# A 64-byte read of every later x chunk, issued early on the GpSimd queue

## The chip, the cores and the metric

The kernel runs on one core of a Trainium2 chip. The metric is the device time of one execution in microseconds (us), median over runs. A run counts as "fast": for a one-core program this only means that it is not more than 1.5% above the fastest run of the same kernel. The profile of an execution covers a "span" that is about 1.7 us shorter than the timed figure. In the views, PE is TensorE, PEld its weight loads, DVE VectorE, ACT ScalarE, POOL GpSimd and SP SyncE; L186 is line 186 of the kernel, and x5 a count.

## The reference, cut to what matters

```
def reference(A_x, A_wqkv, A_wo, B_x, B_w1, B_w2, B_w3, B_w4, gate_w):
    x = A_x                                    # (1, 2048, 640), bfloat16
    g = sigmoid((x * gate_w).sum(-1, keepdims=True))
    a = linear attention over 32 heads of 20: q, k, v = x @ wqkv;  phi(t) = where(t > 0, t + 1, exp(t)) + 1e-6
    b = shifted-mixer block and MLP with two layernorms: w1, w2, w3, w4
    return g * a + (1 - g) * b
    # [cut: the bodies of a and b]
```

The rows of x are taken as 16 chunks of 128 rows. The first stage needs each chunk transposed (`xT`), as the stationary operand of k = x @ wk.

## The kernel before

The parts that matter are the loads at the start, GpSimd's set-up, and the k stage. `sp`, `aq` and `gq` issue DMAs from SyncE, ScalarE and GpSimd.

```python
    def load_x(c0, c1, q=sp):
        q.dma_start(x_sb[:, c0:c1, 0:D], x2[c0 * P:c1 * P, :].rearrange("(c p) d -> p c d", p=P))

    def load_xT(c0, c1):
        sp.dma_start_transpose(xT[:, :, c0 * P:c1 * P], x2[c0 * P:c1 * P, :])

    # [cut: load_wk loads 128 rows of wk]

    load_x(0, 1)
    aq.dma_start(g5[:], gate_w.rearrange("(c p) -> c p", p=P))
    load_wk(sp, 1)
    load_wk(aq, 0)
    load_x(1, 2, aq)
    load_wk(sp, 3)
    load_wk(aq, 2)
    load_wk(sp, 4)
    for c0, c1 in ((2, 3), (3, 4), (4, 6), (6, 8), (8, 12), (12, 16)):
        load_xT(c0, c1)
    sp.dma_start(wq_sb, wqkv_v[:, :, 0:D])
    load_x(2, 8)
    load_x(8, 16)
    sp.dma_start(wv_sb[:], wqkv_v[:, :, 2 * D:3 * D])
    # [cut: the loads of w1, wo, w2, w3]

    nc.gpsimd.memset(mhalf[:], -0.5)
    nc.gpsimd.memset(ident[:], 1.0)
    nc.gpsimd.affine_select(out=ident[:], in_=ident[:], compare_op=ALU.is_equal, fill=0.0,
                            base=0, pattern=[[-1, P]], channel_multiplier=1)
    nc.gpsimd.memset(x_sb[:, :, D:D + 1], 1.0)
    # [cut: other masks, kvT memsets, and copies that wait for w1]
```

Chunks 0 and 1 are loaded as they are and transposed on TensorE. Chunks 2 to 15 come through DMA transposes, in six loads of 1, 1, 2, 2, 4 and 4 chunks. The k stage fills the time of the first loads with warm-up matmuls on ones:

```python
    warmup(5)
    warmup(1, 3 * P)
    kp = pair()
    turns = [(pair(), a, b) for a, b in ((0, 2), (2, DC))]
    # [cut: turn(c) transposes chunk c on TensorE and evacuates it]
    turn(0)
    warmup(1, TS)
    for n, dc in enumerate(k0_order):
        if n == 3:
            turn(1)
        elif 1 <= n < 3:
            warmup(1, 2 * P)
        k_mm(kp, 0, (dc,), first=k0_order[0], last=k0_order[-1])
    k_evac(kp, 0)
    for c in range(1, NCH):
        pt = pair()
        k_mm(pt, c, range(DC))
        k_evac(pt, c)
```

The next stage (`q_unit`) reads `xT` and `wq_sb`; the one after it reads the plain `x_sb`.

Of the kernel before, what the change touches and what calls it, by code (L numbers as in the profile page):

```python
# [9 lines left out]
BF16 = mybir.dt.bfloat16  # L10
# [6 lines left out]
def kernel(  # L17
# [14 lines left out]
    P = 128  # L32
# [3 lines left out]
    NCH = S // P  # L36
# [18 lines left out]
    x2 = A_x.rearrange("b s d -> (b s) d")  # L55
# [5 lines left out]
    const = ctx.enter_context(tc.tile_pool(name="const", bufs=1))  # L61
# [24 lines left out]
    r4 = const.tile([H, NT, TS], BF16)  # L86
    ident = const.tile([P, P], BF16)
    g5 = const.tile([DC, P], BF16)
    g5z = const.tile([P, P], BF16)
    mhalf = const.tile([P, CPT], F32)  # L90
    hmask = const.tile([P, H], F32)
# [24 lines left out]
    sp, aq, gq = nc.sync, nc.scalar, nc.gpsimd  # L116
# [27 lines left out]
    for g in range(4):  # L144
# [6 lines left out]
    nc.gpsimd.memset(ident[:], 1.0)  # L151
    nc.gpsimd.affine_select(out=ident[:], in_=ident[:], compare_op=ALU.is_equal, fill=0.0,
                            base=0, pattern=[[-1, P]], channel_multiplier=1)
    nc.gpsimd.memset(x_sb[:, :, D:D + 1], 1.0)
    nc.gpsimd.memset(hmask[:], 1.0)
    nc.gpsimd.affine_select(out=hmask[:], in_=hmask[:], compare_op=ALU.is_ge, fill=0.0,
# [466 lines left out]
```

## Time and profile before

| | before |
|---|---|
| time, median of 3 runs before the change was run | 264.34 us (264.27 to 264.57) |
| span of the profiled run | 262.6 us |
| TensorE busy | 257.9 us, 98% |
| first k matmul, last k matmul (start) | 4.22 us, 27.29 us |
| chunks 8-11 of xT: landed, first needed | 16.44 us, 16.52 us |

The first fence is from the page of before: the busy time of the engines, two rows of the span in 40 equal slices (each digit is the busy share of a slice in tenths), and the two lines of the chain that ended last.

```profile
PE 257.9 (98%) x1719; PEld 160.0 (61%) x1738; DVE 142.7 (54%) x282; ACT 82.7 (31%) x123; POOL 20.2 (8%) x65
...
PE   8999999999999999999999999999999999999995
...
DMA  7999987016682566600132000051100051100011
...
PE 98%; issue 0%; DVE 0%
PE pp L500 22%; PE pp L467 21%; PE pp L186 9%; PE pp L315 8%; PE pp L451 8%; PE pp L420 8%; PE pp L349 8%; PE pp L243 8%; PE pp L199 1%; PE pp L387 1%; PE pp L475 1%; PE pp L509 1%; PE pp L368 1%; PE pp L258 0%; PE pp L216 0%
```

TensorE bounds the kernel: it is at 9 in all slices but the first and last, and the chain holds no DMA, although the DMA row is at 9 for the first slices. Busy DMA is not a cost where nobody waits for it.

The second fence is the waits view of before, the lines of TensorE that name a DMA or an evacuation (engine, tile, line, what it waited for; us in total, times, longest).

```profile
PEld L216 <- DMA x_sb<-in_A_x_dram: 0.5, 1, 0.5
...
PEld L186 <- DVE xT L219: 0.2, 1, 0.2
PEld L214 <- DMA x_sb<-in_A_x_dram: 0.2, 1, 0.2
```

All three are in the first 6.1 us. No line says that TensorE waited for an `xT<-in_A_x_dram` load, which is what the change is aimed at.

The third fence is the timeline of before, TensorE only, the k stage and its neighbours (start, length, engine, line, operation, tiles, shapes, count).

```profile
4.22 0.93 PE L186 MATMUL pp<-wk_sb,xT 128*128 128x320 bf16 x2
...
5.15 0.68 PE L186 MATMUL pp<-wk_sb,xT 128*128 128x320 bf16 x2
...
5.77 0.44 PE L186 MATMUL pp<-wk_sb,xT 128*128 128x320 bf16 x2
...
6.08 0.45 PE L214 MATMUL pp<-ident,x_sb 128*128 128x128 bf16 x5
...
6.44 21.14 PE L186 MATMUL pp<-wk_sb,xT 128*128 128x320 bf16 x154
...
27.42 4.91 PE L243 MATMUL pp<-xT,hsT 128*128 128x512 bf16 x21
```

From 6.44 us, 154 matmuls run without a break.

Two more readings are of the trace's records, not of a view. The semaphore events say when each load has landed: it raises its semaphore in 16 steps, and the last one counts. The DMA packet records say how long each packet took: a transposed chunk is 640 packets of 256 bytes, the median one 18 ns; but there are bursts in which 12 to 19 packets take from 0.16 to 2.0 us and end together (at 6.36, 9.5, 11.55, 11.95 and 16.35 us). These groups of slow packets are called bursts below.

### The profile page before, as it was taken

Reading aid. Unit: us, or ns where it says so; the run is one execution under the profiler, and the core shown is the slowest. Engines: PE = TensorE matmul, PEld = TensorE weight load, DVE = VectorE, ACT = ScalarE, POOL = GpSimd, SP = SyncE. Lnnn points to the kernel's source line nnn. Section 1 sums busy time; section 2 is a strip of 40 time slices with the busy share of each in tenths; the row PEclk is TensorE's granted clock in tenths of the full one; section 3 lists DMA queues with packets and bytes.
Section 4 is the critical chain, followed back from the end, with each engine's and each line's share of the span. In section 5 each row is a group of like instructions: output and inputs, shape, how many; then the busy total and the mean of one; then the engine's idle time right before and its main releaser. Section 6 shows DMA issues by size and latency. Waiting matters only on the chain.

```text
span 262.6 us, 4246 instructions
## 1 busy us (share of the span) xinstructions
PE 257.9 (98%) x1719; PEld 160.0 (61%) x1738; DVE 142.7 (54%) x282; ACT 82.7 (31%) x123; POOL 20.2 (8%) x65
## 2 busy tenths in 40 slices
PE   8999999999999999999999999999999999999995
PEld 4777555788755644555577555567565577555553
DVE  2788778899947998955403464413356223112132
ACT  1555554321166236522502222412131332142200
POOL 5000050012210040001000001000001000000000
DMA  7999987016682566600132000051100051100011
GB/s 204 197 171 379 364 248 304 0 27 125 125 99 58 111 121 167 235 0 2 25 75 77 25 0 2 0 100 52 50 0 2 1 100 52 50 0 2 0 50 50
DMA packets 45757, 23.98 MB, mean 91 GB/s; under 512 B 35114, under 2 KB 44970, under 8 KB 45738
## 3 DMA queue, kind: packets, MB, share of 16 engines
q1 hardware_dynamic: 45296, 23.22, 35.1%
q10 hardware_dynamic: 442, 0.49, 0.5%
q8 instruction: 13, 0.21, 0.4%
q14 instruction: 6, 0.05, 0.1%
HBM read 12.21 MB, written 2.62 MB: 56 GB/s over the span
## 4 chain that ended last, share of the span: by engine, by line
PE 98%; issue 0%; DVE 0%
PE pp L500 22%; PE pp L467 21%; PE pp L186 9%; PE pp L315 8%; PE pp L451 8%; PE pp L420 8%; PE pp L349 8%; PE pp L243 8%; PE pp L199 1%; PE pp L387 1%; PE pp L475 1%; PE pp L509 1%; PE pp L368 1%; PE pp L258 0%; PE pp L216 0%
## 5 line engine op out<-in xcount | busy, mean ns | idle before, releaser
L467 PE MATMUL pp<-lnxT,w_sb 128*128 128x512 bf16 x249 | 59.8, 379 | 0.6
L500 PE MATMUL pp<-w_sb,h 128*128 128x384 bf16 (+3 forms) x414 | 57.6, 299 | 0.2 <-issue 0.2
L469 ACT ACTIVATE h<-pp 128x1024 bf16<-128x1024 f32 (+1 forms) x28 | 26.9, 961 | 82.2 <-PE pp L467 82.2
L500 PEld LDWEIGHTS <-h 128*128 128x128 bf16 x416 | 38.3, 98 | 19.3 <-issue 1.1
L467 PEld LDWEIGHTS <-w_sb 128*128 128x128 bf16 x260 | 25.4, 98 | 26.8
L514 DVE SCALAR_TENSOR_TENSOR oc<-pp,omg,x 128x640 bf16<-128x640 f32 (+2 forms) x20 | 14.4, 748 | 45.1 <-ACT h2x L478 21.3
L454 DVE SCALAR_TENSOR_TENSOR x<-pp,gate,x 128x640 f32<-128x640 f32 x16 | 13.9, 868 | 29.4 <-PE pp L451 29.4
L178 ACT ACTIVATE e<-pp 128x640 bf16<-128x640 f32 (+1 forms) x26 | 21.5, 826 | 9.6 <-PE pp L243 9.6
L451 PE MATMUL pp<-m_sb,pqT 128*128 128x320 bf16 x160 | 24.3, 299 | 0.0
L420 PE MATMUL pp<-w_sb,hsT 128*128 128x320 bf16 x160 | 23.9, 299 | 0.0
L423 DVE TENSOR_TENSOR x<-pp,x_sb 128x640 f32<-128x640 f32 x16 | 13.1, 820 | 19.7 <-PE pp L420 19.7
L186 PE MATMUL pp<-wk_sb,xT 128*128 128x320 bf16 (+1 forms) x160 | 23.1, 303 | 0.0
L315 PE MATMUL pp<-x_sb,pk 128*128 128x320 bf16 (+1 forms) x160 | 22.0, 300 | 0.0
L243 PE MATMUL pp<-xT,hsT 128*128 128x512 bf16 x98 | 21.6, 379 | 0.1
L315 PEld LDWEIGHTS <-pk 128*128 128x128 bf16 x160 | 18.8, 117 | 3.2
L420 PEld LDWEIGHTS <-hsT 128*128 128x128 bf16 x160 | 15.7, 98 | 8.2
L451 PEld LDWEIGHTS <-pqT 128*128 128x128 bf16 x160 | 15.7, 98 | 7.7
L186 PEld LDWEIGHTS <-xT 128*128 128x128 bf16 x160 | 15.7, 99 | 6.5 <-DVE xT L219 0.2
L349 PE MATMUL pp<-lnxT,w_sb 128*128 128x512 bf16 x76 | 17.9, 379 | 0.2
L243 PEld LDWEIGHTS <-hsT 128*128 128x128 bf16 x100 | 11.8, 118 | 9.7
L285 POOL TENSOR_SCALAR rstd<-mv 128x4 f32<-128x4 f32 (+1 forms) x11 | 3.4, 312 | 153.6 <-DVE mv L291 153.6
L180 DVE SCALAR_TENSOR_TENSOR pk<-pp,e 128x640 bf16<-128x640 f32 x16 | 13.2, 825 | 1.7
(76 smaller groups left out, 189.9 us busy)
## 6 DMA issues: line engine op xcount, KB each, us to landing
out_dram<-oc SPq DMA_DIRECT2D x14, 160.0 KB, 1.8
w_sb<-in_B_w_dram SPq DMA_DIRECT2D x1, 2160.0 KB, 8.4
w_sb<-in_B_w_dram SPq DMA_DIRECT2D x1, 2080.0 KB, 9.9
x_sb<-in_A_x_dram SPq DMA_DIRECT2D x1, 1280.0 KB
x_sb<-in_A_x_dram SPq DMA_DIRECT2D x1, 960.0 KB, 7.4
wo_sb<-in_A_wo_dram SPq DMA_DIRECT2D x6, 160.0 KB, 7.8
hsT<-in_A_wqkv_dram SPq DMA_DIRECT2D x1, 800.0 KB, 5.1
m_sb<-in_A_wqkv_dram SPq DMA_DIRECT2D x1, 800.0 KB, 12.0
```

What stands on the lines that cost most here:

```text
L178: nc.scalar.activation(ev, src, ACT.Exp)
L186: nc.tensor.matmul(pt[:, hf, 0:n], lhsT=xT[:, dc, c * P:(c + 1) * P], rhs=wk_sb[:, dc, hf * HD:hf * HD + n], start=(dc == first), stop=(dc ...
L243: nc.tensor.matmul(pt[:, t % 2, :], lhsT=wq_sb[:, dc, :].rearrange("p (m j) -> p j m", j=DC)[:, j], rhs=xT[:, dc, t * TS:(t + 1) * TS], st ...
L315: nc.tensor.matmul(pt[:, hf, 0:HD + hf], lhsT=w, rhs=x_sb[:, c, hf * HD:(hf + 1) * HD + hf], start=(c == 0), stop=(c == NCH - 1))
L349: nc.tensor.matmul(pt[:, i, :], lhsT=w, rhs=lnxT[t][:, dc, :], start=(dc == 0), stop=(dc == DC - 1))
L420: nc.tensor.matmul(pt[:, hf, 0:HD], lhsT=hsT[:, fc, 2 + c * P:2 + (c + 1) * P], rhs=w2_sb[:, fc, hf * HD:(hf + 1) * HD], start=(fc == 0), ...
L451: nc.tensor.matmul(pt[:, hf, 0:HD], lhsT=pqT[:, j, c * P:(c + 1) * P], rhs=m_sb[:, j, hf * HD:(hf + 1) * HD], start=(j == 0), stop=(j == D ...
L454: nc.vector.scalar_tensor_tensor(x1, pt[:, :, 0:HD], gate[:, c:c + 1], x1, op0=ALU.mult, op1=ALU.add)
L467: nc.tensor.matmul(pt[:, k, :], lhsT=w3_sb[:, dc, fc * P:(fc + 1) * P], rhs=lnT[:, dc, :], start=(dc == 0), stop=(dc == DC - 1))
L469: nc.scalar.activation(h2[:, 2 * i * TS:(2 * i + n) * TS], pt[:].rearrange("p h e -> p (h e)")[:, 0:n * TS], ACT.Gelu_apprx_tanh)
L500: nc.tensor.matmul(dst, lhsT=st[t]["h2"][:, fc * TS + cc * P:fc * TS + (cc + 1) * P], rhs=w4_sb[:, fc, a:b], start=start and fc == 0, stop ...
L514: nc.vector.scalar_tensor_tensor(oc[:, a:b], src, omg[:, c:c + 1], st[t]["x1"][cc][:, a:b], op0=ALU.mult, op1=ALU.add)
```

## The change

Its intent, as the code suggests, is to read a little of every later x chunk while the first chunks are loading, so that whatever makes the first packets of those chunks slow is over by the time the transposed loads reach them. The spare tile is read by nothing.

```diff
@@
     g5 = const.tile([DC, P], BF16)
+    touch = const.tile([NCH - 2, 32], BF16)
     g5z = const.tile([P, P], BF16)
@@
     nc.gpsimd.affine_select(out=ident[:], in_=ident[:], compare_op=ALU.is_equal, fill=0.0,
                             base=0, pattern=[[-1, P]], channel_multiplier=1)
+    gq.dma_start(touch[:], x2.rearrange("(c p) d -> p c d", p=P)[0, 2:NCH, 0:32])
     nc.gpsimd.memset(x_sb[:, :, D:D + 1], 1.0)
```

## The prediction

> **What bounds the kernel.** TensorE. The page gives PE 257.9 us busy of a 262.6 us span (98%), and the chain that ended last is PE for 98%, with no DMA in it. From 6.44 us to the end the matmuls follow each other without a wait that the waits view lists above 0.4 us. Only the first 6.5 us are tied to loads. There the timeline shows PE and its weight load waiting 0.49 us for x chunk 0, 0.25 us for an evacuation of xT, and 0.20 us for x chunk 1; warm-up matmuls fill the rest.
>
> **What the loads look like now.** The semaphore events of the trace give landings. x chunk 1 has 15 of its 16 increments by 5.51 us and the last at 6.03; PE takes it at 6.08. The weight chunk needed next lands at 6.40 (used 6.44), the last one at 6.58 (used about 6.71). So start-up hangs on the loads within 0.05 to 0.15 us. The transposed loads of x chunks 2 to 15 all land before use: chunk 2 at 7.21 (first matmul 8.35), chunks 4-5 at 9.72 (11.07), 6-7 at 12.03 (13.80), 12-15 at 18.67 (21.97). The tightest is 8-11: landed 16.44, used 16.52, 0.08 us to spare. The packet records show bursts of slow packets where the transposes reach new chunks: a median 256-byte packet takes 18 ns, but some 18 of them at 5.8-6.2 us take 0.16 to 0.59 us, with further bursts at 9.0, 10.8, 11.7 and 14.3 us (up to 2.0 us). I read the change as an attempt to take these first-read delays early; that a first read is their cause is a guess.
>
> **What the change does.** It removes nothing. It adds one DMA of 14 x 64 bytes (896 bytes against 24 MB in total), issued from GpSimd after the identity mask, at about 1.35 us. Nothing reads the spare tile. It takes its own completion semaphore, so the built programs of the other engines have the same order and the same waits. GpSimd's remaining set-up (mask work and kvT memset, now done by 4.6 us) slips by the descriptor generation; the Trainium skill, "DMA: Bandwidth & Descriptors", section "Latency and other measured facts", gives about 1 us to first byte on this path. GpSimd then idles 28 us until w1 lands, so the slip is free. By the same page ("Issuing engines are not separate DMA queues") the 14 reads run on the same DMA engines as the start-up loads, so they reach them at an estimated 2.5-3.5 us, amid the weight and x chunk 1 loads.
>
> **On the critical path.** Gain: if the bursts at 5.8-6.2 us shrink, x chunk 1 and the last weight chunks land earlier, worth at most the 0.20 us wait plus about 0.1 us; and the chunk 8-11 load gets spare time that PE does not need. Earlier transposes otherwise buy nothing. Cost: slow first reads among the start-up loads could delay them by up to about 0.5 us, passed on one for one. Expected net: about -0.1 us.
>
> **Prediction.** 264.2 us, 263.6 to 264.8 (8 in 10). Faster by over 2%: 0.005; within 2%: 0.985; slower: 0.01.
>
> **Right or wrong in the profile.** Right: PE busy unchanged within 1 us; the slow packets at 9, 10.8 and 14.3 us fewer or shorter, chunk 8-11 landing before 16 us, yet the first q matmul (27.4 us now) within 0.4 us of its old place. Wrong: the bursts unchanged (the touch warms nothing), or x chunk 1 and the weights landing over 0.5 us later and the whole timeline shifted.
>
> **What would break it.** The load blocking a DMA engine for microseconds at start-up; a PE gap long enough to lower its clock; or a fixed cost outside the span for using the GpSimd queue at all (262.6 span against 264.34 timed).

## The result, and the profile after

| | before | after |
|---|---|---|
| time, median | 264.45 us (264.27 to 264.91, 4 runs) | 264.67 us (264.28 to 264.85, 4 runs) |
| ratio after / before | | 1.0004, 95% interval 0.9986 to 1.0021 |
| span of the profiled run | 262.6 us | 262.9 us |
| last k matmul (start) | 27.29 us | 27.48 us |
| chunks 8-11: landed, first needed | 16.44, 16.52 us | 14.79, 16.71 us |
| chunks 12-15: landed, first needed | 18.67, 21.97 us | 18.59, 22.16 us |

A ratio is the mean time of one kernel's fast runs over that of the other's of the same rounds, so it is not quite the ratio of the medians.

The page of after, the lines that answer to those of before, and the DMA queue that is new:

```profile
PE 258.1 (98%) x1719; PEld 160.3 (61%) x1738; DVE 142.7 (54%) x282; ACT 82.7 (31%) x123; POOL 20.7 (8%) x66
...
PE   8999999999999999999999999999999999999995
...
DMA  7999995016672566700132000051100051100011
...
q0 software_dynamic: 32, 0.00, 0.0%
...
PE 98%; issue 0%; DVE 0%
PE pp L502 22%; PE pp L469 21%; PE pp L188 9%; PE pp L317 8%; PE pp L453 8%; PE pp L422 8%; PE pp L351 8%; PE pp L245 8%; PE pp L201 1%; PE pp L389 1%; PE pp L477 1%; PE pp L511 1%; PE pp L370 1%; PE pp L260 0%; PE pp L218 0%
```

The chain is the same, shifted by two line numbers. The touch is 32 packets (14 of 64 bytes and 18 of 4 bytes); its share rounds to nothing.

GpSimd's timeline, one line of before and then those of after, shows what the touch costs there:

```profile
3.35 1.28 POOL L167 MEMSET kvT<- 128x320 bf16 x4
```

```profile
1.46 0.75 POOL L155 DMA_DIRECT2D touch<-in_A_x_dram  x1
2.21 0.19 POOL L156 MEMSET x_sb<- 128x16 bf16 x1
...
4.19 1.28 POOL L169 MEMSET kvT<- 128x320 bf16 x4
31.71 3.24 POOL L172 COPY w1x<-w_sb 128x32 bf16<-128x32 bf16 x20 [26.24 <-DMA w_sb<-in_B_w_dram]
```

Issuing takes GpSimd 0.75 us; the kvT memset starts at 4.19 us (3.35 before). Then GpSimd waits 26 us for w1 anyway. The DMA view gives 3.7 us from issue to landing, and the packet records put its 64-byte packets at 3.58 to 4.64 us.

TensorE's timeline of after:

```profile
4.31 0.85 PE L188 MATMUL pp<-wk_sb,xT 128*128 128x320 bf16 x2
...
5.16 0.74 PE L188 MATMUL pp<-wk_sb,xT 128*128 128x320 bf16 x2
...
5.91 0.60 PE L188 MATMUL pp<-wk_sb,xT 128*128 128x320 bf16 x2
...
6.35 0.44 PE L216 MATMUL pp<-ident,x_sb 128*128 128x128 bf16 x5
...
6.63 21.14 PE L188 MATMUL pp<-wk_sb,xT 128*128 128x320 bf16 x154
...
27.61 4.70 PE L245 MATMUL pp<-xT,hsT 128*128 128x512 bf16 x20
```

Two things differ. The unbroken run of 154 matmuls starts 0.19 us later and takes exactly as long (21.14 us). And, off TensorE's path, chunks 8-11 landed 1.65 us earlier. Is the second an effect of the touch, and the first its cost? One trace of each cannot tell. That is what the experiments are for.

### The profile page after: what moved, and what is told of

It reads as the page before. It is cut to its first block, busy times and chain, and to the rows that moved or that the text cites. A ratio compares the mean times of both kernels' runs of the same rounds, so it can differ in the third digit from the quotient of the medians.

```text
span 262.9 us, 4248 instructions
## 1 busy us (share of the span) xinstructions
PE 258.1 (98%) x1719; PEld 160.3 (61%) x1738; DVE 142.7 (54%) x282; ACT 82.7 (31%) x123; POOL 20.7 (8%) x66
## 4 chain that ended last, share of the span: by engine, by line
PE 98%; issue 0%; DVE 0%
PE pp L502 22%; PE pp L469 21%; PE pp L188 9%; PE pp L317 8%; PE pp L453 8%; PE pp L422 8%; PE pp L351 8%; PE pp L245 8%; PE pp L201 1%; PE pp L389 1%; PE pp L477 1%; PE pp L511 1%; PE pp L370 1%; PE pp L260 0%; PE pp L218 0%
## 5 line engine op out<-in xcount | busy, mean ns | idle before, releaser
L422 PEld LDWEIGHTS <-hsT 128*128 128x128 bf16 x160 | 15.7, 98 | 8.2
L453 PEld LDWEIGHTS <-pqT 128*128 128x128 bf16 x160 | 15.7, 98 | 7.7
```

What stands on the lines that cost most here:

```text
L422: nc.tensor.matmul(pt[:, hf, 0:HD], lhsT=hsT[:, fc, 2 + c * P:2 + (c + 1) * P], rhs=w2_sb[:, fc, hf * HD:(hf + 1) * HD], start=(fc == 0), ...
L453: nc.tensor.matmul(pt[:, hf, 0:HD], lhsT=pqT[:, j, c * P:(c + 1) * P], rhs=m_sb[:, j, hf * HD:(hf + 1) * HD], start=(j == 0), stop=(j == D ...
```

## The experiments

The theories:

- **A**: a 64-byte read of a chunk makes its later first reads quick, so the loads of 6-7 and 8-11 land earlier. The time is the same only because TensorE had no need of it.
- **B**: those landings move from run to run by themselves; the touch does nothing.
- **C**: the touch delays the start-up loads and costs about 0.2 us.
- **A'**: any extra DMA on GpSimd's queue does what the touch does.

Later came **F** (the longest burst belongs to the 16 KB fetch of TensorE's instructions), **I** (bursts come where a new transposed load begins) and **P** (bursts belong to places in x).

The first four kernels ran on one chip and share 7 runs of before there: 264.31 us (264.04 to 264.76).

### Before once more

No edit.

> The kernel before, unchanged, for the spread of its own landings. Theory A (a 64-byte read of a chunk makes the later first reads of that chunk quick): chunks 6-7 land again near 12.0 us and chunks 8-11 near 16.4 us (within 0.4 us), as in the first trace of before. Theory B (the bursts of slow packets come and go from run to run, whatever the touch does): these landings move by 0.7 us or more against the first trace, and could be as early as the 11.3 and 14.8 us that the changed kernel showed. Both expect a time within 0.1% of before.

Measured: 264.58 us (264.17 to 265.19, 4 runs), ratio 1.0009 (0.9986 to 1.0031). Chunks 6-7 landed at 11.52 us, 8-11 at 16.25. The last k matmul began at 27.59 us, 0.30 us later than in the first trace of the same kernel. So the start-up of one kernel moves by more than the 0.19 us between before and after. For chunks 6-7, A missed its 12.0 us by more than the 0.4 us that it allowed.

### After once more

No edit.

> The changed kernel, unchanged. Theory A: chunks 6-7 land again near 11.3 us and 8-11 near 14.8 us (within 0.4 us). Theory B: they land anywhere between 11.3 and 12.0, 14.8 and 16.5 us. Theory C (the touch delays the start-up loads): the last k matmul starts about 0.2 us later than in the traces of before (27.5 against 27.3 us) and the time is about 0.1% longer; if C is false, these lie within 0.1 us of those of before.

Measured: 264.47 us (264.14 to 264.65), ratio 1.0002 (0.9987 to 1.0017). Chunks 6-7 landed at 11.71 us, 8-11 at 15.10. The last k matmul began at 27.54 us, between the two traces of before. C is not seen. For 6-7 the touch no longer differs (11.71 us with, 11.52 without). For 8-11, A still stood at two traces against two.

### The touch, but from w4

```diff
-    gq.dma_start(touch[:], x2.rearrange("(c p) d -> p c d", p=P)[0, 2:NCH, 0:32])
+    gq.dma_start(touch[:], B_w4.rearrange("(c p) d -> p c d", p=64)[0, 0:NCH - 2, 0:32])
```

> The same extra load in the same place, 14 x 64 bytes, but from w4 (not needed before 100 us) in place of x. Theory A: no help, chunks 6-7 and 8-11 land as in before, near 12.0 and 16.4 us. Rival A' (any DMA on that queue, or the later GpSimd work, changes the bursts, not the addresses read): they land as in the changed kernel, near 11.3 and 14.8 us. Theory C: start-up as late as with the change. Time within 0.2% of before by all.

Measured: 264.39 us (264.18 to 264.77), ratio 1.0002 (0.9986 to 1.0017). Chunks 6-7 landed at 11.87 us, 8-11 at 16.05: as without a touch. So far for A, against A'. The last k matmul began at 27.06 us, earlier than in either trace of before although an extra DMA ran: against C, but weakly, since TensorE's full clock came early in this trace (below).

### A denser touch

Against the kernel after:

```diff
-    touch = const.tile([NCH - 2, 32], BF16)
+    touch = const.tile([8 * (NCH - 2), 32], BF16)
-    gq.dma_start(touch[:], x2.rearrange("(c p) d -> p c d", p=P)[0, 2:NCH, 0:32])
+    gq.dma_start(touch[:], x2.rearrange("(c p) d -> p c d", p=16)[0, 16:8 * NCH, 0:32])
```

> The touch with a row of every 16 (112 x 64 bytes, one each 20 KB) in place of one row of every 128 (one each 160 KB). Theory A: more of the first reads are taken early, so what slow packets the change left (bursts ending at 14.5 and 17.7 us in its trace) go too: chunks 8-11 land near 14 us and 12-15 near 17 us or before, against 14.8 and 18.6. Theory B: no trend. Theory C: with 8 times the packets at start-up the delay grows, the last k matmul 0.3 us or more later than before. The time stays within 0.3% by A and B, since no matmul waits for these chunks.

Measured: 264.53 us (264.25 to 265.68), ratio 1.0014 (0.9988 to 1.0039). Chunks 8-11 landed at 15.48 us, later than with the thin touch, and 12-15 at 17.75, earlier. The last k matmul began at 27.18 us. No trend that A asked for. The touch went out as 16 packets of 448 bytes, and no delay is seen either.

### What the start-up does to the time

These traces settle the 0.19 us. If the time is lost or won only before the last k matmul, then the span less its start must be the same in all. It is, to 0.06 us (us; differences of the rounded columns):

| trace | last k matmul | span | difference |
|---|---|---|---|
| before | 27.29 | 262.61 | 235.32 |
| before, again | 27.59 | 262.91 | 235.32 |
| after | 27.48 | 262.85 | 235.37 |
| after, again | 27.54 | 262.91 | 235.37 |
| touch from w4 | 27.06 | 262.44 | 235.38 |
| denser touch | 27.18 | 262.54 | 235.36 |

The 0.06 us go with the kernel. In all six traces the last matmul ends 232.61 us after the last k matmul began; from there to the end of the span it is 2.71 us in both traces of before and 2.76 to 2.77 us in the four with an extra load. SyncE's extra wait at the end is the reason at hand, not tested alone. So an extra load has a cost, about 0.05 us, far below what the timed runs can show.

The rest of the spread of these six spans is the start-up, and part of that is TensorE's clock. (Longer runs, such as the 265.68 us of the denser touch, left no trace.) Timeline of the second trace of before, and then of the touch from w4, at the same instructions:

```profile
4.51 0.69 PE L186 MATMUL pp<-wk_sb,xT 128*128 128x320 bf16 x2
...
5.21 0.74 PE L186 MATMUL pp<-wk_sb,xT 128*128 128x320 bf16 x2
...
5.96 0.67 PE L186 MATMUL pp<-wk_sb,xT 128*128 128x320 bf16 x2
```

```profile
4.64 0.43 PE L188 MATMUL pp<-wk_sb,xT 128*128 128x320 bf16 x2 [0.21 <-DMA wk_sb<-in_A_wqkv_dram]
...
5.02 0.43 PE L188 MATMUL pp<-wk_sb,xT 128*128 128x320 bf16 x2
...
5.40 0.44 PE L188 MATMUL pp<-wk_sb,xT 128*128 128x320 bf16 x2
```

A pair takes 0.74 us at the half clock and 0.43 to 0.44 us at the full one. Where a trace holds clock events, the full clock was granted at 6.43 us (before, again), 6.24 and 6.37 us (after, both) and 4.48 us (touch from w4). The Trainium skill, "TensorE: Matmul & The Clock Gate", section "Part 1: The HAM clock gate (the "warmup" mystery)", says that the clock rises after a busy window of 3413 ns and that this window "doesn't reset when your kernel starts". The traces agree: TensorE is busy from 0.83 us in all of them, and in these four the grant comes from 3.65 us (4.48 - 0.83) to 5.6 us (6.43 - 0.83) later. Over all twelve traces of this document that hold clock events it is 3.05 to 5.97 us, and the full clock then lasts 256.000, 259.413 or 262.826 us, which are 75, 76 and 77 times 3.4133 us. The 3.05 us (the changed order with the touch, below) is less than a whole window; if the window is as the page says, it was not busy from its start there. The early clock of the last trace did not bring all it could: it then waited for weights until 6.49 us. I read the start-up as bound by the later of two things, the clock and the loads; both move by some tenths of a microsecond between executions of one kernel.

### The order of the k matmuls changed, without and with the touch

To make the landing of chunks 8-11 show in the time, TensorE is made to need them earlier. The touch kernels have the lines of the change besides.

```diff
-    for c in range(1, NCH):
+    for c in (1, 2, 3, 4, 5, 8, 9, 10, 11, 6, 7, 12, 13, 14, 15):
```

Without the touch:

> No touch; the k matmuls take chunks 8-11 directly after chunk 5, before 6 and 7, so TensorE reaches them at about 13.8 us and must wait for their landing. Theory A and the landings seen so far without the x touch (16.44, 16.25, 16.05 us): a wait of 2.2 to 2.7 us, time 266.5 to 267.2 us (before plus 2.2 to 2.7). If transposes had no bearing even when needed, the time would stay at 264.4.

With it:

> The same order with the touch. Theory A and the landings seen with it (14.79, 15.10 us): a wait of 1.0 to 1.4 us, time 265.4 to 265.9, so 1.0 to 1.5 us less than the same order without the touch. Theory B (landings are noise): the same time as without the touch, within 0.3 us.

With the load from w4 instead:

> The same order with the extra load from w4 in place of x. Theory A: as without a touch, 266.3 to 267.2 us. Rival A' (a DMA on that queue or the later GpSimd work is what helps): as with the touch, 265.4 to 265.9.

Measured on another chip, where before had 264.48 us (264.07 to 264.70 in six runs, and one of 267.21):

| order changed | time, median of 4 | ratio to before | chunks 8-11 landed |
|---|---|---|---|
| no touch | 265.85 us (265.69 to 266.78) | 1.0049 (0.9983 to 1.0114) | 15.12 us |
| touch | 266.50 us (266.07 to 268.62) | 1.0078 (1.0012 to 1.0144) | 15.99 us |
| load from w4 | 266.36 us (265.96 to 266.58) | 1.0055 (1.0001 to 1.0108) | 15.60 us |

The runs of 268.62 us (touch) and 267.21 us (before) had a mean granted clock of 0.992 and 0.994, the others 0.999 or 1.000. The medians hardly feel them; the ratios and their intervals do.

The waits view of the order without the touch, TensorE's line for the transposed load, then that of the order with it:

```profile
PE pp L186 <- DMA xT<-in_A_x_dram: 1.0, 1, 1.0
```

```profile
PE pp L188 <- DMA xT<-in_A_x_dram: 2.0, 1, 2.0
```

Now there is a wait where before had none, and it is longer with the touch. A had promised 1.0 to 1.5 us less. A is in trouble: the landing without a touch (15.12) is as early as those that A ascribed to the touch, and the time missed A's 266.5 to 267.2 us.

The pair was run again on a third chip, five rounds:

> The reordered kernel without the touch again, beside the next one on the same chip. Theory B (landings vary from run to run and the touch does not shorten them): median 265.7 to 266.5 us. Theory A would have had 266.5 to 267.2, which the first run of it (265.85) already missed.

> The reordered kernel with the touch. Theory B: within 0.4 us of the same order without the touch, in either direction. Theory A: 1.0 us or more below it. The first pair had it 0.65 us above.

Measured: 266.08 us without (264.87 to 268.06, 6 runs), ratio to before 1.0055 (1.0009 to 1.0102); 265.88 us with (265.22 to 266.76), ratio 1.0042 (1.0006 to 1.0078). Before had 264.57 us there. Chunks 8-11 landed at 14.85 us without and 14.66 us with. The sign has turned, and the difference of the medians, 0.20 us, is far from 1.0. Over all traces with this load whole, the landings of 8-11 are 14.34 (the last kernel below), 14.85, 15.12, 15.60, 16.05, 16.25, 16.44 and 16.46 us without the touch of x, and 14.66, 14.79, 15.10, 15.48 and 15.99 us with it. The means are 15.6 and 15.2 us, the second range lies inside the first: B. A shift of a few tenths is not excluded; one that a kernel could use is not there.

The traces hold a better divider than the touch: the first 16 KB fetch of instructions, which the next experiment explains. In the five of these traces where it began by 14.3 us, 6 to 8 of the load's 16 semaphore steps came, then none for 1.2 to 1.9 us, and the load landed at 15.48 to 16.46 us. (In before they stop at 14.46 and go on at 16.32 us, when the burst beside the fetch ends.) In the eight where it began at 15.06 us or later, the load landed at 14.34 to 15.99 us, at 15.0 us on average without the touch of x and at 15.1 with it. In before the fetch began at 13.68 us and in after at 15.69: the 1.65 us of the first pair go with the fetch.

### An instruction stream that is 34 instructions longer at its start

In every trace so far that had such a fetch by 15.7 us, the packet that took longest began 0.4 to 0.7 us after the start of a 16 KB packet on the instruction queue. These packets come about every 256 TensorE instructions (254 recorded ones on average in the trace of before). To shift them against the loads, the warm-up is cut finer (the same 2944 columns in 23 matmuls for 6). There is no touch.

```diff
-    warmup(5)
-    warmup(1, 3 * P)
+    warmup(23, P)
```

> The kernel before, with the six warm-up matmuls of 512 and 384 columns replaced by 23 of 128 columns (the same 2944 columns), so TensorE's instruction stream is 34 instructions longer at its start. Theory F (the long burst, ending at 15.3 to 17.7 us in every trace, is tied to the 16 KB fetch of TensorE's instructions whose record begins 0.4 to 0.6 us before it): the fetch comes about 2.3 us earlier, near 11.4 us, and the long burst ends near 13.5 us, with no burst over 1 us after 14 us. Rival (the long burst belongs to the first reads of chunk 12): the burst stays where the packets of chunk 12 begin, ending near 16 us, whatever the fetch does. Time within 0.2% of before by both.

Measured: the expectation failed. The first fetch did not come earlier (14.23 us for 13.68), so the end of the burst, at 16.2 us and near the rival's 16, tests neither theory. The second and third fetch did come earlier, at 31.1 and 53.7 us for 34.5 and 56.3. The time was 265.88 us (265.16 to 267.22, 4 runs) for 264.48, not within the expected 0.2%; the ratio is 1.0044 with an interval of 0.9984 to 1.0105, as one run on each side had 267.2. The trace shows where its part of that went, at an unforeseen place. Timeline of before, then of this kernel, at the stage where `gs` is transposed in SBUF by DMA and the `kv` matmuls (line 368 or 367) wait for it:

```profile
69.93 4.63 SPq L319 DMA_TRANSPOSE wk_sb<-gs  x3
...
76.20 1.60 PE L368 MATMUL pp<-wk_sb,m_sb 128*128 128x120 bf16 x30
```

```profile
69.96 6.03 SPq L318 DMA_TRANSPOSE wk_sb<-gs  x3
...
77.61 1.59 PE L367 MATMUL pp<-wk_sb,m_sb 128*128 128x120 bf16 x30 [1.22 <-DMA wk_sb<-gs]
```

The kv matmuls start 1.41 us later and waited 1.22 us for the transposes. The fourth 16 KB fetch is the reason at hand: it began at 70.93 us and took 1.34 us, in the middle of these transposes, and their 256-byte packets, at most 65 ns long just before it, then took up to 1448 ns. In before this fetch came at 77.34 us, after they were done, and the slow packets (up to 1735 ns) fell on a layernorm transpose that nobody was waiting for. Nothing here is read from x. A count over all 14 traces bears this out. In each of the 23 cases where a fetch began amid a DMA transpose (50 or more packets of 256 bytes began 0.2 to 1.0 us after it), the slowest of these packets took 1.2 to 2.0 us. And of the 275 packets of 256 bytes that took over 0.7 us after 18 us, 271 began within 1.4 us after the start of a fetch. So the DMA transposes here that met an instruction fetch were held up, the one above by about 1.4 us, and a change of 34 instructions on TensorE was enough to move one onto the critical path.

### The last two transposed loads cut in four

```diff
-    for c0, c1 in ((2, 3), (3, 4), (4, 6), (6, 8), (8, 12), (12, 16)):
+    for c0, c1 in ((2, 3), (3, 4), (4, 6), (6, 8), (8, 10), (10, 12), (12, 14), (14, 16)):
```

> The kernel before with the last two transposed loads (chunks 8-11 and 12-15) cut into four of two chunks. Measure: the time that each 640 packets of 256 bytes (one chunk) take, 0.57 us when undisturbed; in all ten traces so far the slow groups are the 5th, 7th or 8th, and 11th counted after the first, which begin where the loads of 6-7, 8-11 and 12-15 begin. Theory I (the bursts come where a new transposed load begins): two more slow groups of over 0.3 us excess, where the loads of 10-11 and 14-15 begin. Theory P (they belong to places in x, whether by first read or otherwise): the same places as before, none at 10 and 14. Time within 0.2% of before.

Measured: 264.56 us (264.24 to 265.42), ratio 0.9996 (0.9954 to 1.0039). The groups are in the table below. One new slow group came where the load of 10-11 begins (1.28 us), none at 14-15 (0.57): I right once and wrong once; P wrong at 10. It also removes the thin margin: chunks 8-9 landed at 13.11 us and 10-11 at 15.76, needed at 16.27 and 19.0. The time did not move.

### Chunks 8-11 loaded twice

```diff
     for c0, c1 in ((2, 3), (3, 4), (4, 6), (6, 8), (8, 12), (12, 16)):
+        if c0 == 12:
+            sp.dma_start_transpose(pqT[:, :, 0:TS], x2[8 * P:12 * P, :])
         load_xT(c0, c1)
```

> The kernel before with one transposed load more: chunks 8-11 are loaded a second time, into a part of pqT that nothing has written yet and that is overwritten later, between the loads of 8-11 and 12-15. The rows have been read 3 us before. Theory A (first reads are slow): no burst where the second load of 8-11 begins (its first group takes under 0.75 us), and the burst of about 1 to 2 us comes 2.3 us later, where 12-15 begin. Theory I: a burst of about 1 to 2 us where the second load of 8-11 begins although its rows were just read, and another at 12-15. The load of 12-15 lands 2.5 to 4 us later, near 21 to 22.5 us, used at 22.0: time 264.3 to 265.2.

Measured: 264.74 us (264.49 to 264.87), ratio 0.9997 (0.9956 to 1.0038). The table gives the time of each 640 packets in us, in order of their ends; 0.56 to 0.60 is undisturbed, and "fetch" is the start of the first 16 KB instruction packet.

| trace | 3, 4, 5 | 6, 7 | 8 to 11 | second 8 to 11 | 12 to 15 | fetch |
|---|---|---|---|---|---|---|
| before | 0.67 0.66 0.62 | 1.22 0.58 | 1.72 0.59 0.57 0.68 | | 2.64 0.57 0.57 0.58 | 13.68 |
| after | 0.67 0.59 0.59 | 1.14 0.62 | 1.09 0.70 0.57 0.61 | | 1.62 0.57 0.58 2.06 | 15.69 |
| order, no touch | 0.60 0.60 0.59 | 1.13 0.78 | 1.09 0.83 0.82 0.59 | | 1.47 0.56 0.57 0.76 | 16.76 |
| loads cut in four | 0.62 0.81 0.63 | 1.17 0.58 | 0.99 0.63 1.28 0.58 | | 2.05 0.57 0.57 0.59 | 13.64 |
| 8-11 loaded twice | 0.68 0.58 0.57 | 1.19 0.65 | 1.05 0.63 0.57 0.67 | 1.01 0.79 2.03 0.57 | 0.57 0.57 0.56 0.59 | 15.17 |

The last row is the clearest. Rows of 8-11 that had been read about 3 us before were slow again at the start of their second load (1.01) and at the fetch (2.03, a group that ran from 15.16 to 17.19 us). The first reads of 12-15 were not slow at all (0.56 to 0.59). So first reads are neither enough for a burst nor needed for one, and A falls, mechanism and all.

## Why the prediction was right or wrong

- **What bounds the kernel**: right. TensorE is 98% of the chain before and after, and no trace of either kernel has TensorE waiting for a transposed load.
- **The time**: right, 264.67 us against a predicted 264.2 in 263.6 to 264.8; the expected gain of 0.1 us is not shown. The ratio is 1.0004, and 1.0002 in the repeat.
- **Free on GpSimd, no other engine's program changed**: right on GpSimd, which slipped by 0.84 us (kvT memset 3.35 to 4.19) and then waited 26 us. Not quite right on the others: SyncE got one wait more at the end, and there the traces with an extra load are 0.05 us longer.
- **When the touch reaches the DMA engines**: an estimate of 2.5 to 3.5 us; measured 3.58 to 4.64. The term that was mis-sized is the time to first byte, 2.1 us from the start of the issue (3.58 - 1.46) and not about 1.
- **Gain at start-up, up to 0.3 us**: did not come. The burst before 6.5 us was 18 packets of at most 0.59 us in before and 16 of at most 0.60 us in after.
- **Cost at start-up, up to 0.5 us**: not seen. The start-up of the same kernel moves by 0.30 us (27.29 and 27.59), the two traces of after lie inside that, and those with other touches lie below.
- **First-read delays, called a guess**: wrong. A second read is slow and a first read quick in the kernel that loads 8-11 twice. What the runs show in its place: bursts near the start of several transposed loads in the first 16 us, and packets of 1.2 to 2.0 us beside each 16 KB instruction fetch that met a transpose.
- **The marks of "right" in the profile**: chunks 8-11 before 16 us came true at 14.79, and proved nothing, since without any touch they landed between 14.34 and 16.46 us. The landings go with the time of the first instruction fetch, not with the touch. The mark had been set from one trace. The prediction's "0.08 us to spare" was such a single draw too.

Left open: why bursts come at the starts of some transposed loads (6-7, 8-11) and not others (3, 4-5, and 12-15 in the last kernel); why the first fetch came at 15.1 to 15.7 us in both traces of the changed kernel and in that of the double load, and at 13.4 to 14.2 us in the six others with the usual order of matmuls (it is late in two of three traces with a touch of x and in one of six without, too few to say that the touch moves it); and whether the touch moves the landing of 8-11 by a few tenths of a microsecond.

## What to carry to other kernels

Before hiding a latency, look whether anyone waits for it: the waits view had no line for these loads, so making them faster could gain nothing. To learn whether such a treatment works at all, put it where it shows (here, by changing the order of the matmuls) and repeat the base as often as the variant, because the landing of one DMA moved by 2 us between traces without the touch. Look too for what else differs between two traces before naming a cause: here it was an instruction fetch. And a transfer of a few hundred bytes and a shift of a few dozen instructions are not alike: the first cost about 0.05 us, the second moved an instruction fetch onto a transpose that was on the critical path.

## What the Trainium skill lacked or had wrong

- "DMA: Bandwidth & Descriptors", section "Latency and other measured facts", gives about 1 us to the first byte of a DMA issued from GpSimd. Here it was 2.1 us from the start of the issue (1.46 us) to the first packet (3.58 us), 0.75 us of it GpSimd's own, and 3.7 us to landing, beside busy start-up loads; over all seven traces with such a load, 2.1 to 2.5 us to the first packet.
- The same page, section "Queues, rings and completion order", says that an engine serves its queues in turn and switches only after a whole packet. Neither it nor another page says what an instruction fetch does to DMA transposes. Here each fetch is one packet of 16,384 bytes that took 0.88 to 1.93 us, about every 256 TensorE instructions; in the shifted-stream kernel 256-byte transpose packets went from at most 65 ns to 1448 ns beside it, and the last transpose was about 1.4 us late, and in all 23 such meetings some packets took 1.2 to 2.0 us. That it is the turn-taking at packet ends fits, but no run separates the engines.
- No page mentions the bursts where a transposed load begins: 0.5 to 1.2 us over the 0.57 us that 640 packets need in both traces of before, at the starts of chunks 6-7 and 8-11, with no fetch near.
- "TensorE: Matmul & The Clock Gate" was right on the window that runs free of the kernel's start; here the full clock came 3.05 to 5.97 us after TensorE's first matmul. Not explained by these runs: four runs, two of them of the kernel before, had a mean granted clock of 0.992 to 0.994 over the span and took 267.2 to 268.6 us, 2 to 3 us over their like; none of them left a trace.
